# Chunked linear attention and a feed-forward block on one core: block 0's tokens turned from the two rounded parts of y, both halves of W1 centred by mean products, and all pieces in another order

## The chip, the cores and the metric

The kernel runs on 1 core of one Trainium2 chip. The metric is the device time of the program in microseconds (us); lower is better. Before the change the median of three runs is 186.92 us (186.61 to 187.53).

## The reference

```python
# attention: x (4, 8, 768, 32), a (4, 8, 768), B and C (4, 8, 768, 16), chunks of 32 tokens
for c in range(nc):
    la = log_a[:, :, sl]
    cum = np.cumsum(la, axis=-1)
    L = np.exp(cum[:, :, :, None] - cum[:, :, None, :]) * causal
    M = np.einsum('bhin,bhjn->bhij', Cc, Bc) * L
    y_intra = np.einsum('bhij,bhjd->bhid', M, xc)
    y_inter = np.einsum('bhin,bhnd->bhid', Cc, state) * np.exp(cum)[:, :, :, None]
    y[:, :, sl] = y_intra + y_inter
    state = decay_full[:, :, None, None] * state + np.sum(Bx, axis=2)
# feed-forward on the tokens (4, 768, 256): w_ch1 (256, 1024), w_ch2 (1024, 256)
mu, var = np.mean(x, -1, keepdims=True), np.mean((x - mu) ** 2, -1, keepdims=True)
xn = (x - mu) / np.sqrt(var + 1e-06) * g_ln
ch = np.maximum(xn @ w_ch1, 0.0) @ w_ch2
return x + ch
```

Here the x of the second part is the attention's y with the heads side by side. `w_ch1` and `w_ch2` arrive as float64.

## The kernel before

The 768 tokens are cut into six blocks t = 0 to 5 of 128 tokens; a block holds all 4 batches, so its tiles are 128 partitions by 512 columns. Within a block the attention works on two halves of 64 tokens.

**One block of attention.** `scaled_c` and `parted` (pieces C and cm) scale C by a decay and mask it into two tiles; in block 0 `parted_at_once` (cx) does both steps in one instruction. `scaled_b` (B) scales B. `score` (G) multiplies them, `weighted` (R, four instructions) applies the decays held in WW, `entering` and `value` (Vi, V) build y in PSUM from the incoming state and from x, and `carry` (Z), `kept` (K) and `state_of` (S) step the state. The decays of blocks 0 and 1 come from products with a table of sums (e, cum, msps, emps) and exponentials on ScalarE; those of blocks 2 to 5 from a scan whose result goes through HBM (scr) and comes back as the tile ud.

**Feed-forward.** y is held as two float32r parts, yh (rounded) and yl (the rest), and so are both weights. `hidden` (h) forms one 128-row slice of the hidden layer from six products of 512 columns: yh by the upper part of W1, yh by its lower part, yl by its upper part, each over two halves k of the 256 features. `hidden_h` and `hidden_l` (hh, hl) take the relu and split it again; `outputs` (o) and `outputs_of` (oc) multiply by W2; `finished` (oe) scales by the inverse deviation and adds the token. The mean is taken out of W1 instead of out of y: W1 is multiplied by g and by (1 - 1/256), which the text calls centring. W1 has two column halves c = 0 and 1, each in two row halves k. The float64 words are first turned into float32 by pieces k0, k1, k2, k3, kr and f (magnitude, clamped, shifted, signed, rest, whole).

**The centring before.** Half c = 1 is centred by `centred` (wc): for each k two float32 products of 512 columns, one with the tile gd (built by `centring` from the identity, g and -g/256) and one with gneg. Half c = 0 is centred by `mean_of` (wm): two float32 products for both k, and then one VectorE instruction for each k, `less_mean` (wf). `upper` and `lower` (wh, wl) split the result.

**The tokens.** The deviation and the residual need y with tokens on partitions. Blocks 1 to 5 get it by a 32x32 transpose on VectorE and a trip through HBM (tb, bo, bi). Block 0 has `turned` (T): eight TensorE transposes of the float32 copy y32, which four gathers (y) made.

**Order.** A string ISSUE lists every piece in order; each engine runs its instructions in that order, and waits only for data and for buffers. All DMAs are issued by SyncE's queue (SP). The letter after a colon picks the engine. Pieces `fill` are products of zeros that nothing reads; `pc` is a tiny DMA that reads a loaded tile, so that the queue behind it waits for that load. PSUM has eight banks: five for the attention, three (pool ps_ffn) for e, cum, emps, wc, wm, ph and po in turn; a product into a bank waits until its last reader is done.

## Time and profile before

| | before |
|---|---|
| median of three runs | 186.92 us |
| the profiled execution, its own time | 186.59 us |
| its span (first to last instruction) | 184.8 us |
| TensorE matmul busy | 180.0 us, 97% |
| VectorE / ScalarE / GpSimd busy | 141.9 / 63.0 / 44.3 us |
| DMA | 23.66 MB |

Busy time of TensorE counts overlapping matmuls once, so how long one product holds the engine is read from the starts of neighbouring rows, not from its own duration. A float32 product shows as two records (x2), a transpose or a float32r product as one. A name such as ph or yt is the tile that is written, and w, top and yps drop their numbers.

### The profile page before, as it was taken

How to read it: one execution, taken by the hardware profiler on the slowest of the kernel's cores; microseconds unless marked ns; L12 is line 12 of the kernel's file. 1: busy time of each engine (PE TensorE's matmuls, PEld its weight loads, DVE VectorE, ACT ScalarE, POOL GpSimd, SP SyncE). 2: the span in 40 equal slices, each digit the busy share in tenths (PEclk: the TensorE clock that was granted, in tenths of full speed). 3: DMA queues.
4: the chain of work that ended last, by engine and by line, in shares of the span. 5: the costliest groups of instructions: out<-in, count | busy, mean ns of one | idle time of the engine just before them, and what ended most of it. 6: DMA issues, size and time to landing. Idle time of an engine off the chain costs nothing.

```text
span 184.8 us, 6145 instructions
## 1 busy us (share of the span) xinstructions
PE 180.0 (97%) x2674; PEld 150.1 (81%) x2674; DVE 141.9 (77%) x299; ACT 63.0 (34%) x119; POOL 44.3 (24%) x48
## 2 busy tenths in 40 slices
PE   8899999999999999999999999999999999999992
PEld 6666587877899999989779888888888888888892
DVE  0699988999999978897899789684557855587741
ACT  4699587575332382051208110212011310012000
POOL 0004788563232691014830001000020000000000
PEclk9999999999999999999999999999999999999999
DMA  5997235593896867377243280300070005830011
GB/s 147 311 397 298 58 86 178 176 331 130 249 180 151 233 198 199 96 182 186 28 145 61 82 206 4 85 4 4 0 142 0 0 4 172 188 95 0 4 57 57
DMA packets 37745, 23.66 MB, mean 128 GB/s; under 512 B 23350, under 2 KB 31958, under 8 KB 37718
## 3 DMA queue, kind: packets, MB, share of 16 engines
q1 hardware_dynamic: 37718, 23.27, 45.3%
q8 instruction: 21, 0.34, 0.8%
q14 instruction: 6, 0.05, 0.1%
HBM read 17.36 MB, written 5.90 MB: 126 GB/s over the span
## 4 chain that ended last, share of the span: by engine, by line
PE 93%; DMA 2%; SPq 1%; DVE 1%; issue 1%; DVEq 0%
PE ph L542 37%; PE po L562 15%; PE po L563 8%; PE po L568 8%; PE pp L578 6%; PE yps L424 5%; PE G L397 4%; PE yps L416 3%; PE Z L436 3%; DMA b<-in_bn_dram 2%; PE wc L243 2%; PE idle L597 1%; PE wm L248 1%; SPq L167 1%; PE yt L496 0%
## 5 line engine op out<-in xcount | busy, mean ns | idle before, releaser
L542 PE MATMUL ph<-yh,w 128*128 128x512 f32 x192 | 53.0, 398 | 0.0
L547 ACT ACTIVATE hh<-ph 128x512 fp32r<-128x512 f32 x29 | 17.1, 598 | 75.3 <-PE ph L542 69.0
L562 PE MATMUL po<-w,hh 128*128 128x512 f32 x120 | 42.3, 393 | 0.0
L542 PEld LDWEIGHTS ph<-yh,w 128*128 128x128 f32 x192 | 34.4, 188 | 7.8 <-issue 0.7
L553 DVE SCALAR_TENSOR_TENSOR hl<-ph,hh 128x512 fp32r<-128x512 f32 x48 | 32.4, 686 | 8.2 <-ACT hh L547 7.5
L563 PE MATMUL po<-w,hl 128*128 128x256 f32 x120 | 33.8, 282 | 0.0
L542 PE MATMUL ph<-yl,w 128*128 128x512 f32 x96 | 29.7, 391 | 0.0
L562 PEld LDWEIGHTS po<-w,hh 128*128 128x128 f32 x120 | 22.5, 188 | 5.1 <-issue 0.4
L583 DVE SCALAR_TENSOR_TENSOR o<-po,rstd,ytok 128x256 f32<-128x256 f32 x20 | 9.7, 483 | 18.2 <-PE po L563 14.2
L563 PEld LDWEIGHTS po<-w,hl 128*128 128x128 f32 x120 | 22.7, 189 | 0.2
L542 PEld LDWEIGHTS ph<-yl,w 128*128 128x128 f32 x96 | 18.0, 188 | 3.9
L403 DVE TENSOR_TENSOR R<-G,WW 128x512 f32<-128x512 f32 x24 | 15.4, 680 | 2.1 <-PE G L397 1.6
L549 DVE TENSOR_SCALAR hh<-ph 128x512 fp32r<-128x512 f32 x19 | 12.9, 681 | 2.6 <-PE ph L542 2.6
L568 PE MATMUL po<-w,hh 128*128 128x256 f32 x80 | 14.3, 281 | 0.0
L568 PEld LDWEIGHTS po<-w,hh 128*128 128x128 f32 x80 | 12.3, 188 | 0.4 <-issue 0.2
L383 ACT COPY WW<-wt 32x1024 f32<-32x1024 f32 x10 | 10.4, 1040 | 5.0 <-DVE R L403 4.8
L578 PE MATMUL pp<-w,hh 128*128 128x256 f32 x64 | 11.5, 281 | 0.0
L477 POOL TENSOR_TENSOR yl<-y,yh 128x512 fp32r<-128x512 f32 x3 | 3.9, 1294 | 31.5 <-DVE yh L474 31.5
L568 PE MATMUL po<-w,hl 128*128 128x256 f32 x40 | 11.2, 279 | 0.0
L228 POOL TENSOR_TENSOR top<-top,low 128x512 int32<-128x512 int32 x4 | 5.4, 1362 | 22.6 <-DVE top L217 19.4
L462 POOL TENSOR_TENSOR sbd<-S,cst 128x256 f32<-128x256 f32 x6 | 4.1, 689 | 27.0 <-DVE S L452 27.0
L578 PEld LDWEIGHTS pp<-w,hh 128*128 128x128 f32 x64 | 10.0, 188 | 0.4
(105 smaller groups left out, 263.6 us busy)
## 6 DMA issues: line engine op xcount, KB each, us to landing
raw<-in_w_dram SPq DMA_DIRECT2D x8, 512.0 KB, 6.3
xt<-in_x_dram SPq DMA_DIRECT2D x6, 512.0 KB, 7.1
...
```

The costliest lines, as they stand in the source:

```text
L383: e.copy(WW[rows, :, :, 1].rearrange("p b h k -> p (b h) k"), wt[rows, t].unsqueeze(2).to_broadcast([SUB, NR, SUB]))
L403: nc.vector.tensor_tensor(out=R.rearrange("p b i k -> p b (i k)"), in0=tiles.pop(("G", t, q)).rearrange("p b i k -> p b (i k)"), in1=WW.re ...
L424: nc.tensor.matmul(tiles["y", t, g, f][32 * k:32 * k + 32, b], x[r, b * NH + h], tiles["R", t, h // 2][r, b, h % 2], start=(t + f + b == 0 ...
L542: nc.tensor.matmul(ph, W1[m // 4, k][:, s, mc], v[:, k], start=(i == 0), stop=(i == len(cmb) - 1))
L547: e.activation(h, tiles["ph", t, m], AF.Relu)
L549: e.tensor_scalar(out=h, in0=tiles["ph", t, m], scalar1=0.0, scalar2=None, op0=ALU.max)
L553: nc.vector.scalar_tensor_tensor(out=l, in0=tiles.pop(("ph", t, m)), scalar=0.0, in1=tiles["hh", t, m].bitcast(F32), op0=ALU.max, op1=ALU. ...
L562: nc.tensor.matmul(both, tiles["hh", t, m][:, cols], W2[m // 2,][:, :, (m % 2) * DM:(m % 2 + 1) * DM], start=(m == 0), stop=False)
L563: nc.tensor.matmul(both[:, 0], tiles["hl", t, m][:, cols], W2[m // 2,][:, 0, (m % 2) * DM:(m % 2 + 1) * DM], start=False, stop=(m == MC - 1))
L568: nc.tensor.matmul(po, tiles[v, t, m][:, cols], W2[m // 2,][:, s, (m % 2) * DM:(m % 2 + 1) * DM], start=(n == 0), stop=(n == len(cmb) - 1))
L578: nc.tensor.matmul(tiles["po", t, b], tiles[v, t, m][:, cols], W2[m // 2,][:, s, (m % 2) * DM:(m % 2 + 1) * DM], start=(c + n + b % 2 == 0 ...
L583: nc.vector.scalar_tensor_tensor(out=o, in0=tiles.pop(("po", t, b)), scalar=tiles["rstd", t][:, b], in1=tiles["ytok", t][:, b], op0=ALU.mu ...
```

## The change

Four things change in the code. `centred` and the tile gd go, and half c = 1 of W1 is centred by `mean_of` and `less_mean` like half c = 0. `turned` forms block 0's tokens as ordinary products of yh and of yl with a float32r identity (identr, made by the new piece `ir`), summed in PSUM: sixteen float32r products of 128 columns in place of eight transposes; the four gathers into y32 for block 0 go with it. `hidden` can be issued in two parts: the two products of yh with the upper W1 first, the other four later. And the tile cs gets two buffers. ISSUE lists the pieces in a new order with new engines for some.

```diff
-    gd = hp.tile([P, KC, P], F32, tag="hh", name="gd")
+    identr = cp.tile([P, P], F32R, name="identr")
...
+    def rounded_ones(e=nc.gpsimd):
+        e.tensor_copy(identr, ident) if e is not nc.scalar else e.copy(identr, ident)
...
-            for k in range(KC):
-                e.activation(gd[:, k], ident, AF.Identity, bias=gneg[:, k:k + 1], scale=gt[:, k:k + 1])
...
-    def centred(c, k):
-        w = centre[c, k] = ps_ffn.tile([P, 512], F32, tag="ffn", name=f"wc{c}{k}")
-        for n, j in enumerate((k, 1 - k)):
-            nc.tensor.matmul(w, gd[:, k] if j == k else gneg[:, j:j + 1].to_broadcast([P, P]), f32[1, c, j], start=(n == 0), stop=(n == 1))
...
-        cs = tiles["cs", t] = p1.tile([P, TB], F32, tag="cs", name=f"cs{t}")
+        cs = tiles["cs", t] = p2.tile([P, TB], F32, tag="cs", name=f"cs{t}")
...
-                nc.tensor.transpose(ps[:, v, g * P:(g + 1) * P], tiles["y32", t][:, g, tok], ident)
+                for n, part in enumerate(("yh", "yl")):
+                    nc.tensor.matmul(ps[:, v, g * P:(g + 1) * P], tiles[part, t][:, g, tok], identr, start=(v + g + n == 0), stop=(v + g + n == 3))
...
-    def hidden(t, m):
+    def hidden(t, m, *part):
...
         for i, (s, v, k) in enumerate(cmb):
-            nc.tensor.matmul(ph, W1[m // 4, k][:, s, mc], v[:, k], start=(i == 0), stop=(i == len(cmb) - 1))
+            if not part or (i < KC) == (part[0] == 0):
+                nc.tensor.matmul(ph, W1[m // 4, k][:, s, mc], v[:, k], start=(i == 0), stop=(i == len(cmb) - 1))
...
-ld la, l1, fill 8 256, fill 4 256, fill 2 256, ini, ld sums, ld mask, ld w1 1 0, l2, lr 0, fill 6 256, e 1, x 1, dc 0, fill 5 256, fill 3 64, so,
+ld la, l1, l2, inv, ld sums, fill 2 256, fill 1 512, fill 8 256, ld mask, lr 0, ini, ld w1 1 0, ones, e 1, x 1, W:v 0, ld g, dc 0, lr 1, k0 1 1 0,
```

The first place is VectorE at the start, from the tile of decayed B (bs) to the weighted scores R of block 0. Before:

```order
L363 SCALAR_TENSOR_TENSOR cm_163<-c_158,cst,ud_149 128x512 x2
L367 TENSOR_TENSOR bs_168<-b_166,ud_149 128x512
L217 SCALAR_TENSOR_TENSOR top_147<-raw_123,top_147 128x512
L348 TENSOR_TENSOR cs_223<-c_158,ud_149 128x512
L228 ISA top_147<-top_147,low_211 128x1024
L203 TENSOR_SCALAR top_219<-top_219 128x512
L313 TENSOR_TENSOR mblk<-msum,selt 32x144
L212 TENSOR_SCALAR top_219<-top_219 128x512
L376 TENSOR_TENSOR be_236<-bt_226,pend 128x512
L217 SCALAR_TENSOR_TENSOR top_219<-raw_216,top_219 128x512
L403 TENSOR_TENSOR R_265<-G_175,WW 128x512
```

And now:

```order
L342 TENSOR_TENSOR cs_154<-c_146,ud_148 128x512
L361 TENSOR_TENSOR bs_166<-b_151,ud_148 128x512
L212 TENSOR_SCALAR top_143<-top_143 128x512
L307 TENSOR_TENSOR mblk<-msum,selt 32x144
L217 SCALAR_TENSOR_TENSOR top_143<-raw_127,top_143 128x512
L228 ISA top_143<-top_143,low_170 128x1024
L203 TENSOR_SCALAR top_178<-top_178 128x512
L397 TENSOR_TENSOR R_230<-G_197,WW 128x512
L397 TENSOR_TENSOR R_242<-G_194,WW 128x512
L212 TENSOR_SCALAR top_178<-top_178 128x512
L397 TENSOR_TENSOR R_255<-G_196,WW 128x512
```

The two cm have gone to ScalarE, be to GpSimd, and the R stand earlier: between them and behind them lie the steps of the second W1 tile (top_219 before, top_178 now).

The second place is TensorE at the start, between the sums of decays (e, cum, msps) and the scores G. Before:

```order
L293 MATMUL cum_133<-cf,lr_126 128x128 x4
L597 MATMUL idle<-const-float32-0.0 128x256
L597 MATMUL idle<-const-float32-0.0 128x64
L306 MATMUL msps<-cst,la 32x8 x6
L597 MATMUL idle<-const-float32-0.0 128x512
L293 MATMUL cum_170<-cf,lr_156 128x128 x4
L397 MATMUL G_175<-cm_163,bs_168 64x128
```

And now:

```order
L287 MATMUL cum_136<-cf,lr_123 128x128 x4
L300 MATMUL msps<-cst,la 32x8 x6
L595 MATMUL idle<-const-float32-0.0 128x256
L275 MATMUL e_181<-la,cf 128x192
L287 MATMUL cum_183<-cf,lr_141 128x128 x4
L391 MATMUL G_194<-cm_164,bs_166 64x128
```

The product e_181 (e 0) stood behind G before and stands ahead of it now, in the bank of cum_136, so it waits until ScalarE has read that tile twice; two fills have moved behind G.

The third place is TensorE where block 0's feed-forward begins. Before:

```order
L243 MATMUL wc_409<-top_219,gd 128x512
L243 MATMUL wc_409<-top_147,gneg 128x512
L248 MATMUL wm_422<-top_287,gneg 128x512
L248 MATMUL wm_422<-top_298,gneg 128x512
L496 MATMUL yt_425<-cst,y_373 128x128 x4
L496 MATMUL yt_434<-cst,y_373 128x128 x4
L436 MATMUL Z_450<-xt_234,be_236 32x64 x16
```

And now:

```order
L242 MATMUL wm_423<-top_279,gneg 128x512
L242 MATMUL wm_423<-top_288,gneg 128x512
L540 MATMUL ph_426<-yh_361,w_364 128x512
L540 MATMUL ph_426<-yh_361,w_416 128x512
L540 MATMUL ph_429<-yh_361,w_364 128x512
L540 MATMUL ph_429<-yh_361,w_416 128x512
L491 MATMUL yt_432<-identr,yh_361 128x128
L491 MATMUL yt_432<-identr,yl_362 128x128
```

The first four products of ph stand ahead of the turned tokens yt, which are now float32r products of the two parts; the pair yh, yl comes eight times.

## Rows read from the trace of the kernel before

**Rows 1.** All waits of TensorE: total us, times, longest

```profile
PE idle L597 <- PEq L688: 0.8, 1, 0.8
PE cum L293 <- ACT msum L309: 0.6, 1, 0.6
PE G L397 <- DVE bs L367: 0.2, 1, 0.2
```

**Rows 2.** Busy time by stretch: length, busy us (count) per engine, clock, DMA

```profile
10.09:24.40 14.31, 14.31 (x381) 8.85 (x381) 14.12 (x31) 11.28 (x30) 6.76 (x8) 1.00 0.59 222
24.40:181.60 157.20, 157.16 (x2253) 134.72 (x2248) 122.76 (x260) 45.56 (x80) 37.33 (x36) 1.00 0.44 114
```

**Rows 3.** Timeline of TensorE at the start: start us, length us, instruction, count [idle before]

```profile
0.78 3.75 PE L597 MATMUL idle<-const-float32-0.0 128*128 128x256 f32 x8 [0.78 <-PEq L688]
...
4.93 1.06 PE L293 MATMUL cum<-cf,lr 128*128 128x128 f32 x8
5.82 0.77 PE L597 MATMUL idle<-const-float32-0.0 128*128 128x256 f32 x4
...
10.09 1.21 PE L397 MATMUL G<-cm,bs 32*64 32x128 f32 x64 [0.20 <-DVE bs L367]
...
13.47 0.65 PE L436 MATMUL Z<-xt,be 64*32 64x64 f32 x32
...
14.48 1.13 PE L243 MATMUL wc<-top,gd 128*128 128x512 f32 x2
...
16.45 0.69 PE L416 MATMUL yps<-c,sbd 32*64 32x64 f32 x32
...
18.66 1.13 PE L243 MATMUL wc<-top,gd 128*128 128x512 f32 x2
...
20.48 1.88 PE L248 MATMUL wm<-top,gneg 128*128 128x512 f32 x4
22.20 1.04 PE L496 MATMUL yt<-cst,y 128*128 128x128 f32 x8
23.16 1.30 PE L436 MATMUL Z<-xt,be 64*32 64x64 f32 x96
24.40 1.19 PE L542 MATMUL ph<-yh,w 128*128 128x512 f32 x4
...
27.34 1.21 PE L397 MATMUL G<-cm,bs 32*64 32x128 f32 x64
```

**Rows 4.** The chain that ended last: start us, us, what

```profile
67.23 2.80 PE po L568 x24
...
159.54 10.89 PE ph L542 x48
```

**Rows 5.** Timeline of ScalarE

```profile
6.52 0.67 ACT L198 ACTIVATE top<-raw 128x512 f32<-128x512 f32 x1 [1.06 <-DMA raw<-in_w_dram]
7.09 0.59 ACT L299 ACTIVATE ud<-cum 128x512 f32<-128x512 f32 x1
...
23.37 1.34 ACT L356 ACTIVATE cm<-cs,cst 128x512 f32<-128x512 f32 x2 [2.10 <-POOL cs L348]
```

**Rows 6.** Timeline of VectorE

```profile
13.85 2.46 DVE L403 TENSOR_TENSOR R<-G,WW 128x512 f32<-128x512 f32 x4
16.24 0.40 DVE L203 TENSOR_SCALAR top<-top 128x512 f32<-128x512 f32 x1
...
22.40 0.75 DVE L252 SCALAR_TENSOR_TENSOR top<-top,gt,wm 128x512 f32<-128x512 f32 x1
```

**Rows 7.** DMA issues of the page: count, size, median us to landing

```profile
raw<-in_w_dram SPq DMA_DIRECT2D x8, 512.0 KB, 6.3
```

**Rows 8.** Timeline of SyncE's queue: start us, time to issue, DMA

```profile
4.00 0.43 SPq L157 DMA_DIRECT2D raw<-in_w_dram  x1
...
28.73 3.05 SPq L144 DMA_DIRECT2D ud<-scr  x2
```

**Rows 9.** Timeline of GpSimd: the wait for block 2's decays

```profile
32.75 1.28 POOL L348 TENSOR_TENSOR cs<-c,ud 128x512 f32<-128x512 f32 x1 [0.42 <-DMA ud<-scr]
```

More of the change, by code (lines that the diff above doesn't have):

```diff
@@ L232, in centring @@
             e.activation(gneg, gt, AF.Copy, scale=-1.0 / DM)
-            for k in range(KC):
-                e.activation(gd[:, k], ident, AF.Identity, bias=gneg[:, k:k + 1], scale=gt[:, k:k + 1])
         else:
             e.tensor_scalar(out=gneg, in0=gt, scalar1=-1.0 / DM, scalar2=None, op0=ALU.mult)
-            for k in range(KC):
-                e.tensor_scalar(out=gd[:, k], in0=ident, scalar1=gt[:, k:k + 1], scalar2=gneg[:, k:k + 1], op0=ALU.mult, op1=ALU.add)
-    def centred(c, k):
-        w = centre[c, k] = ps_ffn.tile([P, 512], F32, tag="ffn", name=f"wc{c}{k}")
-        for n, j in enumerate((k, 1 - k)):
-            nc.tensor.matmul(w, gd[:, k] if j == k else gneg[:, j:j + 1].to_broadcast([P, P]), f32[1, c, j], start=(n == 0), stop=(n == 1))
     def mean_of(c):
@@ L534, in inverse @@
         nc.vector.reciprocal(rstd, rstd)
-    def hidden(t, m):
+    def hidden(t, m, *part):
         yh, yl = tiles["yh", t], tiles["yl", t]
-        ph = tiles["ph", t, m] = ps_ffn.tile([P, TB], F32, tag="ffn", name=f"ph{t}{m}")
+        if ("ph", t, m) not in tiles:
+            tiles["ph", t, m] = ps_ffn.tile([P, TB], F32, tag="ffn", name=f"ph{t}{m}")
+        ph = tiles["ph", t, m]
         cmb = [(s, v, k) for s, v in ((0, yh), (1, yh), (0, yl)) for k in range(KC)]
@@ L606, in linear_attention_ffn @@
     do = dict(
-        ld=load, pc=after, fill=fill, fillb=fill_small, az=restart, ini=initial, inv=cleared, ones=masks, gm=centring,
+        ld=load, pc=after, fill=fill, fillb=fill_small, az=restart, ini=initial, inv=cleared, ones=masks, gm=centring, ir=rounded_ones,
         lr=logs_repeated, dc=since_middle, du=decay_from_middle, rcl=rest_clipped, ru=rest_since, riv=rest_last, rd=rest_till, ro=rest_out, C=scaled_c, cm=parted, cx=parted_at_once, B=scaled_b, c2=inter, be=ended,
@@ L610, in linear_attention_ffn @@
         W=decays, G=score, R=weighted, Vi=entering, V=value, Z=carry, K=kept, S=state_of, sb=diagonal,
-        k0=magnitude, k1=clamped, km=bounded, k2=shifted, k3=signed, kr=rest, f=whole, wc=centred, wm=mean_of, wf=less_mean, wh=upper, wl=lower,
+        k0=magnitude, k1=clamped, km=bounded, k2=shifted, k3=signed, kr=rest, f=whole, wm=mean_of, wf=less_mean, wh=upper, wl=lower,
         y=gathered, yh=upper_y, yl=lower_y, uy=upper_of, ly=lower_of, T=turned, tc=tokens, tb=blocks_turned, bo=blocks_out, bi=blocks_in, st=stats, ag=aggregate, rs=root, rc=inverse,
```

72 lines of the change are left out of this document (36 added, 36 removed).

## Prediction

> **What bounds the kernel.** I read TensorE's waits first: there are three, 1.6 us together, and none behind the first G [rows 1]. The table by stretch says the same: from the first G to the first ph TensorE is busy for 14.31 of 14.31 us, and from there to its last product for 157.16 of 157.20 us [rows 2]. So from 10.1 us on nothing ends later than TensorE's own queue. A faster VectorE or ScalarE buys nothing; the change can gain only by products that are gone, or by an earlier start of the dense part, and every new wait of TensorE costs its full length. The second stretch holds the products for all six blocks, and these stay the same in number and size. What has to be priced is the road to them. VectorE, too, is busy for 14.12 of the first stretch's 14.31 us [rows 2], so there the two engines run side by side, and I follow both.
>
> **Prices.** From start to start a float32 product of 512 columns takes 0.86 us (wm: 20.48 to 22.20 for two). The four of wc took 14.48 to 16.45 and 18.66 to 20.48, 3.79 us [rows 3]. Float32r products take 0.227 us at 512 columns (10.89 / 48) and 0.117 at 256 (2.80 / 24) [rows 4]; the straight line through both gives 0.062 at 128, where the trace has none. Vi and V together take 2.21 us, G by its own length 1.2, Z and emps 1.01, the two Z behind the turned tokens 1.24 [rows 3]. The first h behind such small products costs 0.1 more, and the six products of one h 1.4 to 1.5: twelve products fill 24.40 to 27.34 [rows 3].
>
> **What goes from TensorE.** Two wc pairs, 3.79 us, are replaced by one wm pair, 1.72: 2.07 saved. The turned tokens are eight transposes now, 0.96 us (22.20 to 23.16), and become sixteen products, 16 x 0.062 = 0.99 by the line: nothing gained or lost. The bound from above is the price of a plain float32 product of 128 columns, (5.82 - 4.93) / 4 = 0.22 us [rows 3], 3.5 us in all; from below sixteen products cannot cost under nothing, which would gain 0.96. I take the line, since both its points are float32r. The Trainium skill (TensorE: Matmul & The Clock Gate, section "Back-to-back issue gap") gives about 81 ns per product for a stream of weight load and product at 128 columns; by it the sixteen would take 1.3 us and the sum would be 0.3 us worse. The same page (section "Terms") calls transpose mode four times faster for FP32, which speaks against giving it up; here the transposes' 0.12 us stand against 0.22 for plain float32, under a factor of two, and float32r needs no such help.
>
> **The first step, to G.** In the old order G waits for bs on VectorE, behind two cm there, and starts at 10.09 [rows 1, 3]. In the new one the decay tile ud is ready at 7.68 as before (7.09 + 0.59), cs takes some 0.7 on VectorE, like the R or wf [rows 6], until 8.4, and the two cm 1.34 on ScalarE [rows 5], until 9.8; bs is done by 9.1 beside them. G starts at about 9.85, 0.25 earlier. TensorE gets nothing done meanwhile: e 0 waits for both readings of cum (the second ends near 8.2), and fills of 512 and 64 columns have gone behind G, so it idles some 1.8 us ahead of G against 0.8 before [rows 1].
>
> **The second step, to the last float32 product.** Behind G come fills of 512, 64 and 256 columns, emps, Z, and fills of 512 and 256: with half a float32 product's 0.86 for each 256 columns, and 0.1 at two changes of shape, that is 1.2 + 1.5 + 1.0 + 1.3 = 5.0, so TensorE is at the first product of wm 1 at 14.9 and through it at 15.75. The second needs the tile top of W1's lower row half. Its load is now one place later in SP's queue: landing was 4.0 + 6.3 = 10.3 by the median [rows 7, 8], and I take 10.5 (between 10.3, if only the full queue counts, and 10.8, if the delay is passed on whole). On ScalarE it is then k0 to 11.2; on VectorE k1 (0.4), four R at 0.6 with a k2 between, k3 0.6, another k1, and f 0.7 [rows 6]: 11.2 + 0.4 + 2.8 + 0.6 + 0.4 + 0.7 = 16.1. So wm 1 waits 0.3 us and ends at 17.0; Vi and V end at 19.2, against 18.66 before. VectorE goes on from 16.0 with k2, k1, k2, two k3, two wf (0.7 each) and f: 0.4 x 3 + 1.2 + 1.4 + 0.7 = 4.5, so the second product of wm 0 starts at 20.45 instead of 20.1, and wm 0 ends at 21.3, against 22.20 before.
>
> **The third step, to block 1's G.** Then come four h products (1.0), the turned tokens with a change of shape (1.1), Z (1.24) and ten h products (2.4 with the extra change): 21.3 + 5.8 = 27.1. By then fourteen h products are done. The old order is at the same G at 27.34 with twelve; the two are worth 0.46. **Gain: 0.24 + 0.46 = 0.7 us.** The four inputs of this stretch, the rest yl, the lower part of W1, the second wf of c = 0 and the next block's cm, come from VectorE and ScalarE 0.1 to 0.5 us ahead of TensorE by the same adding. The gathers for block 0, four on ScalarE, and the two gd were covered by TensorE's queue already, so their going is worth nothing by itself. The wf pair that VectorE gains (2 x 0.7) is already in the 4.5 us.
>
> **The rest.** Behind 27 us I take the old rate, since the products are the same and the old stretch has no waits. A bank of ps_ffn is free again after its hl, which by my adding comes 0.5 to 3 us ahead of need up to Z of block 2. I cannot read from any row that the order of blocks 2 to 5 is as free of waits; each that appears is a loss.
>
> **Sum.** 186.59 (the profiled execution) - 0.7 = 185.9. The median of the runs stands 0.33 above that execution, so I forecast 186.2 for the median, 0.4% under 186.92. About 0.5%, 0.93 us, is what a measurement of this kernel can tell from no change.
>
> **Rivals.**
> *More of the saving arrives.* If VectorE and the load are each some 0.3 us earlier than I added them, both wm waits go (0.3 + 0.35), and the gain is 1.3 us: 185.6. If even the idle time ahead of G were no longer than before, it would be 2.1: 184.8. For it: VectorE's slots scatter by 0.1 us, and I add some twenty. Against it: VectorE is full in that stretch. Chance 0.36 for a gain over 0.93.
> *The turned tokens run at the float32 price.* Sixteen at 0.22 make 3.5 us, 2.5 more, with all of h behind them: 188.7. For it: no row has float32r at 128 columns. Against it: the two sizes that are there lie on one line. It decides from 0.10 us a product on, where the gain is gone. Chance 0.10.
> *A wait that the old order had on GpSimd holds VectorE.* Block 2's cs needs ud, which goes through HBM; GpSimd waited for it, 0.42 us, until 32.75, and ud was issued at 28.73 [rows 8, 9]. It is VectorE's now, ahead of yh of block 1 and of the hl that frees a bank. By my adding VectorE comes to it at 31.8 and the bank is needed 1.5 us after its hl would end, so a landing at 32.75 still costs TensorE nothing; beyond 33.3 each us costs one. If ud takes the 6.3 us of a weight load [rows 7] instead of the 4 it took, TensorE loses 1 to 2: 187.2 to 188.2, slower. For it: larger loads stand close behind it in SP's queue. Against it: they are issued later. Chance 0.08.
> *The clock falls.* The granted clock is 1.00, 2.4 GHz, in both stretches [rows 2]; but the first four fills of 256 columns took 3.75 us, over 0.9 each, where half of a 512 takes 0.43 [rows 3], so the start is at the lower level, 1.2 GHz. If the 1.8 us of idling ahead of G bring that level back, G and what follows take double for as long as those fills did, 3.75 us, of which half is lost: 188.1. Against it: 0.8 us of idling there did nothing before. Chance 0.06.
>
> **Numbers.** My forecast, a gain of 0 to 0.93 us, has 0.40; its own range is 185.9 to 186.9. Faster by over 0.5% has 0.36, slower by over 0.5% 0.10 + 0.08 + 0.06 = 0.24. Under 185.1 lies only the full saving, some 0.05; above 188.0 the float32 price and the far end of the others, some 0.14. So the range is 185.1 to 188.0.
>
> **What would show it.** G at 9.8 to 9.9 with TensorE idle by 1.8 us ahead of it; a TensorE wait of some 0.3 us in wm 1 for top and one in wm 0; wc gone; yt sixteen records in about 1.0 us; block 1's G at 27.1; no waits behind. I am wrong if yt takes over 1.6 us, if ph or po wait for VectorE's yh or hl, or if any stretch behind G is below clock 1.00.

## The result and the profile after

The changed kernel takes 188.61 us (median of nine runs, 187.41 to 189.33); beside it the kernel before took 186.66. The ratio is 1.009, with an interval of 1.0071 to 1.0108: slower by 0.9%, where I had forecast 186.2 us, in a range of 185.1 to 188.0. The profiled execution took 188.66 us, its span is 186.9 us against 184.8. TensorE is busy for 180.6 us of it, VectorE for 140.1, ScalarE for 70.0, GpSimd for 40.2.

All waits of TensorE in the changed kernel (total us, times, longest); [rows 1] answers to it:

```profile
PE e L275 <- ACT msum L303: 0.8, 1, 0.8
PE Z L430 <- DMA xt<-in_x_dram: 0.8, 1, 0.8
PE idle L595 <- PEq L686: 0.8, 1, 0.8
PE wm L242 <- POOL top L228: 0.4, 1, 0.4
PE G L391 <- ACT cm L350: 0.2, 1, 0.2
```

Two waits are new behind G: Z waits for xt's load, and wm for a tile that GpSimd writes. The first is not in the prediction. The second is there in part: the prediction had a wait in wm 0, but at its second product and for VectorE (and one in wm 1, which did not come). The timeline of TensorE at the start, to be laid beside [rows 3]:

```profile
9.97 1.21 PE L391 MATMUL G<-cm,bs 32*64 32x128 f32 x64 [0.20 <-ACT cm L350]
...
14.32 0.65 PE L430 MATMUL Z<-xt,be 64*32 64x64 f32 x32 [0.79 <-DMA xt<-in_x_dram]
...
16.30 2.04 PE L242 MATMUL wm<-top,gneg 128*128 128x512 f32 x4
18.27 0.69 PE L410 MATMUL yps<-c,sbd 32*64 32x64 f32 x32
18.90 1.48 PE L418 MATMUL yps<-R,xt 64*32 64x64 f32 x128
20.78 2.32 PE L242 MATMUL wm<-top,gneg 128*128 128x512 f32 x4 [0.40 <-POOL top L228]
22.54 1.49 PE L540 MATMUL ph<-yh,w 128*128 128x512 f32 x4
23.87 0.22 PE L491 MATMUL yt<-identr,yh 128*128 128x128 f32 x1
23.92 0.27 PE L491 MATMUL yt<-identr,yl 128*128 128x128 f32 x1
...
25.69 1.31 PE L430 MATMUL Z<-xt,be 64*32 64x64 f32 x96
...
29.46 0.85 PE L391 MATMUL G<-cm,bs 32*64 32x128 f32 x38
```

The reader is to see three things. wm 0 starts at 20.78, no earlier than the old 20.48, although TensorE has a float32 pair less ahead of it; its second product, the last two of the four records, starts 1.20 us later still, where 0.96 would do (what the first product behind V takes in the kernel before, from 18.66 to 19.62). The same view from 21.95 us on:

```profile
21.98 1.12 PE L242 MATMUL wm<-top,gneg 128*128 128x512 f32 x2
```

The sixteen turned products take 1.82 us (23.87 to 25.69), 0.113 each. And block 1's G comes at 29.46 with fourteen h products done; the old order was there at 27.34 with twelve, which with two more (0.46) is 27.8. So 1.7 us of the 2.1 by which the span is longer are there before G.

The timeline of VectorE in the changed kernel, ahead of wm 0's inputs:

```profile
14.21 1.35 DVE L217 SCALAR_TENSOR_TENSOR top<-raw,top 128x512 int32<-128x512 int32 x1
...
18.30 1.29 DVE L217 SCALAR_TENSOR_TENSOR top<-raw,top 128x512 int32<-128x512 int32 x2
19.51 1.40 DVE L246 SCALAR_TENSOR_TENSOR top<-top,gt,wm 128x512 f32<-128x512 f32 x2
20.82 1.10 DVE L228 CUSTOM_DVE_ANT_0 top<-top,low 128x1024 uint16<-128x1024 uint16 x1
```

And that of GpSimd:

```profile
13.97 1.04 POOL L365 TENSOR_TENSOR c<-cs,em 128x512 f32<-128x512 f32 x1
19.13 1.59 POOL L228 TENSOR_TENSOR top<-top,low 128x512 int32<-128x512 int32 x1 [4.12 <-DVE top L217]
...
20.76 0.61 POOL L438 TENSOR_TENSOR K<-S,emt 128x256 f32<-128x256 f32 x1
```

wm 0's first product needs the sum f of W1[0,0] (L228 on GpSimd, until 20.72), its second the f of W1[0,1] (L228 on VectorE, until 21.92). One k3 (L217) takes 1.35 us where two others take 1.29 together, and that f takes 1.10 where such a one takes 0.69 elsewhere; in both cases GpSimd is in an operation of its own (c at 13.97, K at 20.76). The experiments turn on that.

A second profile of the same kernel, taken later, shows how much of this is one execution's.

> The changed kernel unaltered, profiled a second time. If Z's 0.8 us wait for xt was one execution's (the other kernels with the same start and the same order of loads had none), Z starts at 13.3 to 13.6 without it, wm 0 still starts at 20.3 to 20.8 behind GpSimd's f, its second product at 21.5 to 22.0 behind VectorE's, and block 1's G at 29.0 to 29.5. If the wait belongs to the order of loads, it is there again with 0.5 us or more.

It took 187.29 us (span 185.5; the kernel before 186.47 beside it). Its waits of TensorE behind the first product:

```profile
PE wm L242 <- POOL top L228: 0.5, 1, 0.5
PE G L391 <- ACT cm L350: 0.2, 1, 0.2
```

And wm 1 and wm 0 in its timeline, the second product of wm 0 in a view that starts behind the first:

```profile
15.52 1.91 PE L242 MATMUL wm<-top,gneg 128*128 128x512 f32 x4
...
19.96 2.32 PE L242 MATMUL wm<-top,gneg 128*128 128x512 f32 x4 [0.49 <-POOL top L228]
...
21.15 1.12 PE L242 MATMUL wm<-top,gneg 128*128 128x512 f32 x2
```

Z's wait is gone, the wait of wm for GpSimd is there again; the second product starts 1.19 us behind the first. The first G stands at 10.05, that of block 1 at 28.64.

The second profile lets the 2.07 us be followed that TensorE is spared. From G to wm 1 the way is 5.47 us (10.05 to 15.52), where the old order took 4.39 to its first wc (10.09 to 14.48): 1.1 us more, since more fills stand there. At wm 0, 0.49 and 0.23 us are waits. So wm 0 ends only some 0.2 us earlier than the old one. Then the turned tokens take 0.85 us more than the old transposes, and G of block 1 is 0.8 us behind the old order's 27.8.

Both profiles show that loss of 0.8 us. What comes on top differs: the runs of the changed kernel span 185.5 to 187.6 us, those of the old one mostly 184.6 to 185.6. In the first profile it is Z's wait of 0.8 ahead of G and 0.4 behind it; the median run is as long as that one, but whether it loses its time in the same places isn't shown.

### The profile page after: what moved, and what is told of

Same layout as the page of the kernel before. It is cut to its first block, busy times and chain, and to the rows that moved or that the text cites. A ratio compares the mean times of both kernels' runs of the same rounds, so it can differ in the third digit from the quotient of the medians.

```text
span 186.9 us, 6145 instructions
## 1 busy us (share of the span) xinstructions
PE 180.6 (97%) x2678; PEld 149.7 (80%) x2678; DVE 140.1 (75%) x292; ACT 70.0 (37%) x133; POOL 40.2 (22%) x42
## 4 chain that ended last, share of the span: by engine, by line
PE 87%; DMA 6%; DVE 3%; SPq 1%; issue 1%; ACT 0%
PE ph L540 37%; PE po L560 15%; PE po L566 8%; PE po L561 8%; DMA raw<-in_w_dram 6%; PE pp L576 6%; PE yps L418 4%; PE G L391 3%; PE yps L410 3%; PE Z L430 2%; PE yt L491 1%; DVE top L228 1%; DVE top L217 1%; SPq L167 1%; PE wm L242 1%
## 5 line engine op out<-in xcount | busy, mean ns | idle before, releaser
L540 PE MATMUL ph<-yh,w 128*128 128x512 f32 x192 | 53.9, 400 | 0.0
L545 ACT ACTIVATE hh<-ph 128x512 fp32r<-128x512 f32 x35 | 20.9, 597 | 61.5 <-PE ph L540 59.1
L547 DVE TENSOR_SCALAR hh<-ph 128x512 fp32r<-128x512 f32 x13 | 8.9, 683 | 2.2 <-PE ph L540 1.6
L438 POOL TENSOR_TENSOR K<-S,emt 128x256 f32<-128x256 f32 x8 | 5.5, 687 | 21.4 <-DVE S L446 21.4
L518 DVE BATCH_NORM_STATS2 st<-ytok 128x6 f32<-128x256 f32 x24 | 9.5, 411 | 0.0
L576 PE MATMUL pp<-w,hl 128*128 128x256 f32 x32 | 8.9, 279 | 0.0
```

What stands on the lines that cost most here:

```text
L518: nc.vector.bn_stats(out=st, in_=tiles["ytok", t][:, b])
L540: nc.tensor.matmul(ph, W1[m // 4, k][:, s, mc], v[:, k], start=(i == 0), stop=(i == len(cmb) - 1))
L545: e.activation(h, tiles["ph", t, m], AF.Relu)
L547: e.tensor_scalar(out=h, in0=tiles["ph", t, m], scalar1=0.0, scalar2=None, op0=ALU.max)
L576: nc.tensor.matmul(tiles["po", t, b], tiles[v, t, m][:, cols], W2[m // 2,][:, s, (m % 2) * DM:(m % 2 + 1) * DM], start=(c + n + b % 2 == 0 ...
```

## Experiments

Each ratio is to the kernel before, with its interval; the changed kernel has 1.009. A diff of the string ISSUE shows only the pieces around those that move. The expectations speak of four theories. **A:** the read on SP's queue, moved ahead of the loads, makes them late, and that sets the time. **B:** a turned product costs 0.113 us, its weight load, and the sixteen are paid in full. **C:** the chain of VectorE and GpSimd to wm 0's inputs, not TensorE's queue, sets wm 0, so that what TensorE is spared ahead of it becomes waiting. **D:** a VectorE operation with its operands in SBUF is held while GpSimd works, and that lengthens the chain of C.

**The loads.** The read that holds SP's queue goes back behind the loads (in the changed kernel), or ahead of them (in the old one).

```diff
-sp, pc 4 w1 1 0, ld bt 0, be 0,
+sp, ld bt 0, be 0,
...
-ld x 0, ld w1 0 0, k2 1 1 1, ld w1 0 1,
+ld x 0, ld w1 0 0, k2 1 1 1, ld w1 0 1, pc 4 w1 1 0,
```

> The changed kernel with one thing undone: the small read of W1[1,0] that holds SP's queue stands behind the loads of xt and of the upper half of W1 again. Theory A (the held queue made xt, and the loads behind it, late): xt lands at 12.6 instead of 14.2, Z of block 0 starts at about 13.1 without the 0.8 us wait, W1's c = 0 tiles come 1.2 us earlier too, wm 0 ends at 21.4 instead of 22.5, block 1's G starts at about 28.2 instead of 29.5, and the time is 1.2 us less than the changed kernel's: 0.2 to 0.7 us above before, a ratio of 1.001 to 1.004. Rival (the transfers share one bandwidth, so that starting one earlier makes another late): block 1's G stays at 29.3 to 29.5 and the ratio at 1.009.

Measured: 1.0109 (1.0085 to 1.0132). xt's load is issued at 5.44 instead of 7.83, Z no longer waits for it, and nothing is won. The earlier loads seem not to be free: W1's first tile reaches ScalarE at 7.05 instead of 6.59, and G starts at 10.35 instead of 9.97. Two later kernels with the early load of xt have 10.12 and 10.40, the kernels with the held queue 9.82 to 10.10, one execution each. And wm 0 waits for GpSimd as before. The clock fell in this profile (last section), but was at 0.997 or above in the other five runs, which took 188.5 to 189.1 us. Theory A falls as the cause of the time; Z's wait is real but not what sets wm 0.

```diff
-C:v 0, f:v 1 1 0, ld bt 0, k1 1 1 1,
+C:v 0, f:v 1 1 0, pc 4 w1 1 0, ld bt 0, k1 1 1 1,
...
-R 0 2, pc 4 w1 1 0, S 0 0,
+R 0 2, S 0 0,
```

> The kernel before with the small read of W1[1,0] on SP's queue moved ahead of bt's load, where the changed kernel has it, and nothing else. Theory A: bt and xt land 1.5 us later (12.8 and 14.2 instead of 11.2 and 12.6), be on VectorE and Z on TensorE wait for them, Z of block 0 starts at 14.3 or later instead of 13.47, VectorE's work for W1 is pushed back by as much, and the time is 1 to 2 us above before, a ratio of 1.005 to 1.011. Rival (the loads have slack in the old order): within 0.3 us, 1.000 to 1.002.

Measured: 1.0034 (1.0020 to 1.0047), between the two. Z starts at 13.57, 0.1 later than before, and G of block 1 at 27.50; the profiled run loses its 0.9 us at 55 us, in pp, where the profile names no releaser. That doesn't bear out theory A either; the 0.3% that the interval leaves has no cause shown.

**The price of the turned tokens.** In the changed kernel yl's eight products are left out; in the old one the turned tokens alone are changed, and stand behind the last yl, which they now read.

```diff
-                for n, part in enumerate(("yh", "yl")):
+                for n, part in enumerate(("yh",)):
```

> The changed kernel with block 0's tokens turned from yh alone, eight float32r products instead of sixteen (the yl part is left out of them). Theory B (each costs 0.113 us, what loading its 128 weight columns takes, not the 0.062 of the line): the eight take 0.9 us instead of 1.8, block 1's G starts 0.9 us earlier, and as TensorE is full behind it the time is 0.9 us less than the changed kernel's, a ratio of 1.004. Rival one, the price of the prediction (0.062, the rest of the 1.8 us being change of shape): 0.5 us less, 1.0065. Rival two (the wait for W1's parts behind them takes it back): G of block 1 unmoved, 1.009.

Measured: 1.0051 (1.0027 to 1.0076). The row of the eight in that kernel, and the next:

```profile
23.50 1.00 PE L491 MATMUL yt<-identr,yh 128*128 128x128 f32 x8
24.43 1.30 PE L430 MATMUL Z<-xt,be 64*32 64x64 f32 x96
```

0.93 us for eight, 0.116 each with the change of shape, and the time falls by 0.0039 x 186.7 = 0.7 us: what theory B expects, though the intervals of the two kernels overlap.

```diff
-                nc.tensor.transpose(ps[:, v, g * P:(g + 1) * P], tiles["y32", t][:, g, tok], ident)
+                for n, part in enumerate(("yh", "yl")):
+                    nc.tensor.matmul(ps[:, v, g * P:(g + 1) * P], tiles[part, t][:, g, tok], identr, start=(v + g + n == 0), stop=(v + g + n == 3))
...
-uy:v 0 0 0, wl:v 1 1 0, ly 0 0 0, ly 0 1 0, wf 0 0,
+uy:v 0 0 0, ly 0 0 0, ly 0 1 0, T 0 0, T 0 1, wl:v 1 1 0, wf 0 0,
```

> The kernel before with the turned tokens alone changed: sixteen float32r products from yh and yl behind the last yl, no gathers of block 0's y on ScalarE. Theory B: yt takes 1.82 us instead of 0.97, with a wait of at most 0.3 us ahead for yl; TensorE is full from there on, so the time is 0.85 to 1.1 us above before, a ratio of 1.0045 to 1.006. Rival, the price of the prediction (sixteen in 1.0 us): 1.000 to 1.002.

Measured: 1.0078 (1.0044 to 1.0113). yt takes 2.22 us (22.18 to 24.40), 0.35 of it a wait, and from G to G the order is 0.83 us longer (28.62 - 10.54 against 27.34 - 10.09). That is theory B's size, and the interval shuts out the 1.000 to 1.002 of the prediction's price. The profiled run is longer than its kernel's median: of the 2.9 us by which its span exceeds the old one's, 0.83 are these, 0.45 lie ahead of G, and 1.4 are two waits without a releaser, in ph (0.4) and pp (1.0).

**The mean products alone.** The kernel before with only the centring changed.

```diff
-k0 1 0 1, wc 1 0, kr 1 0 0,
+k0 1 0 1, wm 1, wf 1 0, kr 1 0 0,
...
-f:v 1 0 0, wc 1 1, y 0 0 0,
+f:v 1 0 0, wf 1 1, y 0 0 0,
```

> The kernel before with the centring alone changed: wm 1 in place of the first wc pair, no second wc pair, and the two wf of c = 1 on VectorE, one right behind wm 1, one where the second pair stood. Theory C (VectorE, full in that stretch, takes the place of TensorE as the bound): VectorE has 1.3 us more to do, f of W1[0,0] is done at 20.6 as TensorE has been idle from 18.6 on, wm 0 starts at 20.6 with a wait of some 2 us ahead of it, block 1's G is 0 to 1.0 us later than the old 27.34, and the ratio is 1.000 to 1.006. Rival (the 2.07 us of TensorE's work come out at the end): wm 0 at 18.7, G at 25.3, ratio 0.989.

Measured: 1.0109 (1.0082 to 1.0136), worse than either theory. The timeline of TensorE at wm 0:

```profile
21.17 3.10 PE L246 MATMUL wm<-top,gneg 128*128 128x512 f32 x4 [2.36 <-DVE top L228]
```

And of VectorE, the f that it waits for:

```profile
20.34 0.69 DVE L228 CUSTOM_DVE_ANT_0 top<-top,low 128x1024 uint16<-128x1024 uint16 x1
```

The 2.07 us that TensorE no longer works it waits, and 0.3 more, for VectorE's f; the wf pair comes on top for all that follows, and G of block 1 is at 30.00. In the old order those inputs come hardly sooner than they are needed: the f of GpSimd, for the second product (about 21.3 there), ends at 21.09.

```profile
19.50 1.59 POOL L228 TENSOR_TENSOR top<-top,low 128x512 int32<-128x512 int32 x1 [3.15 <-ACT em L324]
```

Part of the time of the mean products alone is the clock's, though: the page's PEclk falls to 0.7 to 0.8 in two slices after the wait, and of the six runs the four with a mean clock of 0.989 to 0.991 take 188.87 to 189.74 us, the two at 1.000 187.90 and 188.55.

Does VectorE alone keep the saving in? Here four of its operations ahead of wm 0 are left out.

```diff
-k1 1 0 0, k2 1 0 0, k3 1 0 0, k1 1 0 1, k2 1 0 1, k3 1 0 1, kr 1 0 1,
+k1 1 0 0, k1 1 0 1, kr 1 0 1,
```

> The kernel before with the mean products alone (b2), and four operations of VectorE left out ahead of wm 0: k2 and k3 of W1[0,0] and of W1[0,1] (their weights keep their clamped top words instead of the value, so the output is off). Theory C (VectorE's chain alone keeps the 2.07 us of TensorE from coming out): 2.0 us less on VectorE, so f of W1[0,0] ends at 18.8 to 19.2 instead of 21.0, wm 0 starts at 18.8 to 19.3 with a wait under 0.5 us instead of 2.4, its second product at 19.9 to 20.3, block 1's G at 26.0 to 26.6, and the ratio falls from b2's 1.011 to 0.992 to 0.997, under before. Rival (the loads, ScalarE or the gathers hold the stretch as well): ratio 1.000 or above.

Measured: 1.0017 (0.9994 to 1.0040), 1.7 us under the kernel it is derived from (part of which is that kernel's clock), though not under before, where 0.992 to 0.997 was expected. The timeline of TensorE in this kernel:

```profile
18.57 2.17 PE L246 MATMUL wm<-top,gneg 128*128 128x512 f32 x4
...
21.55 0.65 PE L434 MATMUL Z<-xt,be 64*32 64x64 f32 x32
22.80 1.12 PE L434 MATMUL Z<-xt,be 64*32 64x64 f32 x64 [0.60 <-issue]
```

Of VectorE:

```profile
20.85 1.51 DVE L259 TENSOR_TENSOR w<-top,w 128x512 fp32r<-128x512 f32 x1
22.29 0.74 DVE L486 TENSOR_TENSOR yl<-yps,yh 128x256 fp32r<-128x256 f32 x2
```

And of GpSimd:

```profile
20.54 1.28 POOL L346 TENSOR_TENSOR cs<-c,ud 128x512 f32<-128x512 f32 x1
```

wm 0 starts 2.6 us earlier and without a wait, 1.9 us ahead of the old order's, as theory C has it. Then Z stops, and takes 2.30 us instead of 1.24: by the code it needs banks that the yl free, and the yl stand behind a wl that takes 1.51 us while GpSimd makes cs. G of block 1 comes at 26.80, 0.5 ahead of the old one, and the span is the old 184.8: the rest of the lead goes behind G, with no wait that the profile shows. So VectorE's chain is what wm 0 waits for; that the 2.07 us would come out at the end without it is not shown.

**VectorE held by GpSimd.** The same pattern, made on purpose: two additions on GpSimd that nothing needs, in the old order where it idles.

```diff
+        e.tensor_tensor(out=idler, in0=src[:, :512], in1=src[:, 512:1024], op=ALU.add)
...
-c2:p 0,
+c2:p 0, xx, xx,
```

> The kernel before with two additions on GpSimd, behind its c2 of block 0, where it idles from 16.35 to 19.5 us: each adds two stretches of WW (128x512, 1.3 us alone) into a tile that nothing reads. Theory D (an operation of VectorE whose operands lie in SBUF alone doesn't proceed while GpSimd's runs, it ends about its own length after it; one that reads PSUM isn't held): k2 and one or two of the k behind it take 1.0 to 1.5 us instead of 0.4 to 0.7, f of W1[0,0] ends 1.5 to 2.2 us later than 19.95, wm 0 and all behind it come 1.0 to 2 us later, and the ratio is 1.005 to 1.011. Rival (the two engines run side by side, and what was read as holding was something else): no operation of VectorE is longer, ratio 1.000.

Measured: 1.0100 (1.0068 to 1.0131). VectorE in this kernel:

```profile
16.70 1.40 DVE L212 TENSOR_SCALAR top<-top 128x512 int32<-128x512 int32 x1
18.14 1.65 DVE L217 SCALAR_TENSOR_TENSOR top<-raw,top 128x512 int32<-128x512 int32 x1
```

GpSimd in it, the two additions:

```profile
16.32 2.91 POOL L378 TENSOR_TENSOR idler<-WW 128x512 f32<-128x512 f32 x2
```

The same two in the kernel before, with GpSimd idle:

```profile
16.68 0.43 DVE L212 TENSOR_SCALAR top<-top 128x512 int32<-128x512 int32 x1
17.14 0.69 DVE L217 SCALAR_TENSOR_TENSOR top<-raw,top 128x512 int32<-128x512 int32 x1
```

k2 and k3 are 0.97 and 0.96 us longer, wm 0 starts at 22.06 instead of 20.48, G of block 1 at 29.20. Theory D holds. The Trainium skill (SBUF — State Buffer, section "Who interferes with whom") states the rule: a VectorE instruction with two SBUF inputs, or in a two-port mode, and a GpSimd instruction that reads SBUF exclude each other, and the later "fully blocks". The trace agrees (1.40 and 1.65 us beside GpSimd, 0.43 and 0.69 without), and also where an operand is in PSUM: the R of [rows 6] take 0.6 each, though GpSimd's f runs from 14.07 to 15.34. It speaks against this change, and the prediction overlooked it.

**Trying to bring wm 0's inputs forward.** In the changed kernel the two f go ahead of what stands in front of them; then both to VectorE.

```diff
-k0 1 0 1, k2 1 0 0, kr 1 0 1, kr 1 0 0, k1 1 0 1, k2 1 0 1, fill 6 256, k3 1 0 0, f 1 0 0, k3 1 0 1,
+kr 1 0 0, k0 1 0 1, k2 1 0 0, k3 1 0 0, f 1 0 0, kr 1 0 1, k1 1 0 1, k2 1 0 1, fill 6 256, k3 1 0 1,
...
-wf 1 0, Vi 0, V 0 0,
+f:v 1 0 1, wf 1 0, Vi 0, V 0 0,
...
-wf 1 1, az, f:v 1 0 1, pc 2 w1 0 0,
+wf 1 1, az, pc 2 w1 0 0,
```

> The changed kernel with the sixteen products kept and the two sums f of W1's upper half put ahead of what stood in front of them: GpSimd's f of W1[0,0] (1.6 us) starts behind a k3 that VectorE does 1.3 us earlier, and VectorE's f of W1[0,1] goes ahead of the two wf. Theory C (wm 0 is set by these two sums, not by TensorE's queue or by the loads): wm 0's first product starts at 19.5 to 19.9 instead of 20.4 to 20.8 with no wait, the second follows without the 0.2 us gap, wm 0 ends at 21.3, block 1's G comes about 1.0 us earlier, and the ratio to before is 1.0025 to 1.005. Rival (the loads of W1's upper half, late behind the held queue, set it): k1 of W1[0,0] starts at 15.3 to 16.1 as before and nothing in front of it is won, wm 0 stays at 20.4, and the ratio at 1.007 to 1.009.

Measured: 1.0175 (1.0141 to 1.0209). VectorE in this kernel:

```profile
17.71 1.46 DVE L212 TENSOR_SCALAR top<-top 128x512 int32<-128x512 int32 x1
19.20 0.98 DVE L217 SCALAR_TENSOR_TENSOR top<-raw,top 128x512 int32<-128x512 int32 x1
20.32 1.33 DVE L228 CUSTOM_DVE_ANT_0 top<-top,low 128x1024 uint16<-128x1024 uint16 x1
```

And GpSimd:

```profile
17.49 1.32 POOL L228 TENSOR_TENSOR top<-top,low 128x512 int32<-128x512 int32 x1 [3.57 <-DVE top L217]
...
18.86 0.78 POOL L438 TENSOR_TENSOR K<-S,emt 128x256 f32<-128x256 f32 x1
19.60 1.50 POOL L370 TENSOR_TENSOR be<-bt,pend 128x512 f32<-128x512 f32 x1
```

The clock fell in this execution (0.55 from 23.50 to 28.00 us), behind the rows shown here. Moved forward, GpSimd's f, K and be meet k2, k3 and f on VectorE instead of the two wf, which read PSUM: each is held, 2.0 us together. wm 0's first product came at 19.43 as expected, the second only behind VectorE's f.

```diff
-k3 1 0 0, f 1 0 0, k3 1 0 1, ld bt 1,
+k3 1 0 0, f:v 1 0 0, k3 1 0 1, f:v 1 0 1, ld bt 1,
...
-wf 1 1, az, f:v 1 0 1, pc 2 w1 0 0,
+wf 1 1, az, pc 2 w1 0 0,
```

> The changed kernel with both sums f of W1's upper half on VectorE, each right behind its k3, so that GpSimd has no long operation there. Theory C and D together (wm 0 is set by GpSimd's 1.6 us for the one f and by the other, held behind GpSimd's K): f of W1[0,0] ends at 19.5 and that of W1[0,1] at 20.7 instead of 20.4 to 20.7 and 21.6 to 21.9, wm 0 has no wait for GpSimd, its second product starts at 20.7 to 21.0 instead of 21.6 to 22.0, and block 1's G comes 0.5 to 0.8 us earlier: ratio 1.005 to 1.0065 against the changed kernel's 1.009. Rival (the two wf that come 0.6 us later hold wh and the first h): G unmoved, 1.009.

Measured: 1.0171 (1.0129 to 1.0213). GpSimd, free of f, took K and be earlier, and be (17.26, 1.32 us) held a k2 for 0.75.

With that, the read of SP's queue behind x's load, the k0 of W1[0,0] ahead of Z, and VectorE's f of W1[1,1] ahead of the next k1:

```diff
-k3 1 0 0, f 1 0 0, k3 1 0 1,
+k3 1 0 0, k3 1 0 1, f:v 1 0 0, f:v 1 0 1,
...
-sp, pc 4 w1 1 0, ld bt 0, be 0,
+sp, ld bt 0, be 0,
...
-ld x 0, ld w1 0 0, k2 1 1 1,
+ld x 0, pc 4 w1 1 0, ld w1 0 0, k2 1 1 1,
...
-du 1 1, Z 0 0, R 0 1, S 0 0, k0 1 0 0,
+du 1 1, k0 1 0 0, Z 0 0, R 0 1, S 0 0,
```

> The changed kernel, sixteen products kept, with all that wm 0 waits for made early: the read that holds SP's queue behind xt's load, ScalarE's k0 of W1[0,0] ahead of S, VectorE's k3 and f of W1[1,1] ahead of k1 of W1[0,0], both f of the upper half on VectorE and ahead of the two wf. If the loads, VectorE's order and GpSimd together are the whole of what held wm 0, its first product starts when V ends, at 19.4 to 19.9, without a wait, wm 0 ends at 21.2 to 21.6 instead of 22.2 to 22.5, the first four h have no wait, block 1's G starts at 27.8 to 28.3, and the ratio is 1.000 to 1.003, the rest being the turned tokens. Rival (something else, such as h's own inputs, takes the wait over): wm 0 early, but G at 29 or later and the ratio at 1.007 or above.

Measured: 1.0176 (1.0138 to 1.0214). The k0 and the loads were early, wm 0 started at 20.75 all the same: be again held a k2 (1.30 us instead of 0.42), and TensorE waited 1.0 us for VectorE's f.

With transposes instead of the sixteen products, and gathers on ScalarE, in the changed order and then in that of the run above:

```diff
+                nc.tensor.transpose(ps[:, v, g * P:(g + 1) * P], tiles["y32", t][:, g, tok], ident)
...
-wh 1 1 1, ld c 1, ir:a, W 1, wm 0,
+wh 1 1 1, ld c 1, y 0 0 1, y 0 1 1, y 0 0 0, y 0 1 0, W 1, wm 0,
```

> The changed kernel with block 0's tokens turned as before: y gathered by four copies on ScalarE (in the place of the rounded identity, ahead of the copies of WW) and eight transposes. Theory B (a turned product costs 0.113 us as a transpose does, and there were sixteen of them): yt takes 0.97 us instead of 1.82, block 1's G comes 0.85 us earlier, the time is 0.8 us under the changed kernel's, a ratio of 1.0045 to before. Rival (ScalarE's 1.0 us of copies delays WW and the tokens, and with them the statistics or block 1's R): the ratio stays at 1.009.

Measured: 1.0125 (1.0096 to 1.0155). The four copies start only at 23.26: ScalarE is done with wh at 21.6 and waits 1.66 us, by the profile for VectorE's yl. So yt waited 0.7 us for y. The rival came true.

```diff
-uy 0 0 1, wh 1 1 0, ld as,
+uy 0 0 1, y 0 0 1, y 0 0 0, uy 0 0 0, wh 1 1 0, ld as,
...
-wh 1 1 1, ld c 1, ir:a, W 1, wm 0,
+wh 1 1 1, y 0 1 1, y 0 1 0, em 1, ld c 1, W 1, wm 0,
```

> The kernel of e5 with the tokens turned by eight transposes again, the four copies of y on ScalarE between its copies of yh. Theory B: 0.85 us less of TensorE's time than in e5, all of it in front of a full queue, so 0.85 us less in all: block 1's G at 27.0 to 27.4 with fourteen h done, and a ratio of 0.996 to 0.999, faster than both kernels. Rival (ScalarE's copies come late, as where they stood behind wh): yt waits for y, and the ratio is that of e5 or above.

Measured: 1.0148 (1.0105 to 1.0192), a median of 189.52 us against the 190.14 of the kernel that it is derived from, which the intervals don't tell apart; the second h waited 1.0 us for ScalarE's em, which had moved behind the copies of y. And the old order with VectorE relieved by GpSimd (and wh of the first half later):

```diff
-C:v 0, f:v 1 1 0, ld bt 0,
+C 0, f 1 1 0, ld bt 0,
...
-k0 1 0 1, wc 1 0, kr 1 0 0,
+k0 1 0 1, wm 1, kr 1 0 0,
...
-f:v 1 0 0, wc 1 1, y 0 0 0,
+f:v 1 0 0, wf 1 0, wf 1 1, y 0 0 0,
```

> The kernel before with the mean products alone, and VectorE relieved where it is full: cs of block 0 and f of W1[1,0] on GpSimd, which idles till 14 us there, and both wf of c = 1 behind f of W1[0,0]. Theory C: with 1.2 us taken off VectorE and the two wf out of the way, f of W1[0,0] is done at about 19.5, wm 0 starts at 19.5 to 19.7 instead of 20.48, with a wait of some 1 us left ahead of it, and what was won (0.7 to 0.9 us) stays to the end: a ratio of 0.995 to 0.996. Rival (the saving of the centring never comes out, since the loads and ScalarE are at the limit too): 0.999 to 1.003.

Measured: 1.0124 (1.0102 to 1.0146). cs and f on GpSimd held VectorE's k3 (9.71, 1.75 us) and mblk (11.84, 1.37 us; 0.29 in the kernel before): what was taken off VectorE came back as holds. None of these six beats either kernel.

**Slack or a full queue ahead of wm 0?** The changed kernel with both wc pairs back and no wf of c = 1.

```diff
-ld x 1, wm 1, wf 1 0, Vi 0,
+ld x 1, wc 1 0, Vi 0,
...
-wf 1 1, az, f:v 1 0 1, pc 2 w1 0 0, V 0 1,
+az, f:v 1 0 1, pc 2 w1 0 0, V 0 1, wc 1 1,
```

> The changed kernel with the two wc pairs back for c = 1 and no wf of it on VectorE, all else as in the changed kernel (the identity's load and gd a little earlier): TensorE has 2.07 us more to do, VectorE 1.33 us less. Theory C (TensorE has that much slack ahead of wm 0, since it waits there for VectorE and GpSimd): wm 0 starts at 21.2 to 21.5 without a wait instead of 20.4 to 20.8 with one, the first four h have no wait, block 1's G comes at 29.4 to 29.9, and the ratio is 1.009 to 1.012. Rival (TensorE's queue is the bound, as the prediction had it for V and what follows): 1.7 to 2.1 us more, 1.018 to 1.020.

Measured: 1.0220 (1.0197 to 1.0242). The run tells nothing apart: gd on ScalarE put k0 of W1[0,0] off until 15.88, and VectorE's chain with it. So it was repeated with gd out of the way, k0 at 14.46.

```diff
-sp, pc 4 w1 1 0, ld bt 0,
+sp, ld id, pc 4 w1 1 0, ld bt 0,
...
-du 1 1, Z 0 0, R 0 1, S 0 0, k0 1 0 0, k3 1 1 1,
+gm:a, Z 0 0, R 0 1, S 0 0, k0 1 0 0, du 1 1, k3 1 1 1,
```

> As the run with the two wc pairs back in the changed kernel, but with the identity loaded ahead of bt and gd made on ScalarE where it idles, so that ScalarE's S and k0 of W1[0,0] are not pushed back by gd as they were there (1.0 us). Theory C (TensorE has slack ahead of wm 0 in the changed kernel, since it waits there for VectorE and GpSimd): k1 of W1[0,0] at 15.3 as in the changed kernel, V ends at 19.4 to 19.8, wm 0 starts at 21.2 to 21.6, 0.6 to 1.0 us later than in the changed kernel although TensorE has 2.07 us more to do, and the ratio is 1.010 to 1.014. Rival (TensorE's queue is the bound): wm 0 at 22.4 or later with every start of VectorE as in the changed kernel, ratio 1.018 or above.

Measured: 1.0230 (1.0186 to 1.0274), the rival's ratio and 2.6 us over the changed kernel. The timeline of TensorE at wm 0:

```profile
21.47 1.88 PE L250 MATMUL wm<-top,gneg 128*128 128x512 f32 x4
```

There is no wait. That is 0.7 us later than in the first profile of the changed kernel, but 1.5 later than in the second, with 2.07 more on TensorE ahead of it: the slack is 0.6 us there, about the wait of 0.49, and 1.4 at most. So theory C holds for a part only. In the new order most of what the mean products save does reach wm 0, and with the pairs back it is lost again. Behind wm 0 the second h waits 0.5 us for a wl, the last reader of a wc bank, and there are waits behind G in Z and po without a releaser.

Last, less work for VectorE in the new order:

```diff
-k0 1 0 1, k2 1 0 0, kr 1 0 1, kr 1 0 0, k1 1 0 1, k2 1 0 1, fill 6 256, k3 1 0 0, f 1 0 0, k3 1 0 1, ld bt 1,
+k0 1 0 1, kr 1 0 1, kr 1 0 0, k1 1 0 1, fill 6 256, f 1 0 0, ld bt 1,
```

> The changed kernel with k2 and k3 of W1[0,0] and W1[0,1] left out (their weights keep their clamped top words instead of the value, so the output is off): 2.0 us less on VectorE ahead of wm 0, GpSimd's f of W1[0,0] bound by ScalarE's rest (18.3) instead of by VectorE. Theory C and D: that f ends at 19.9, VectorE's f of W1[0,1] is held by it and ends at 20.5 instead of 21.6 to 21.9, wm 0 starts at 19.9 and its second product at 20.8, the first four h have no wait, block 1's G comes at 28.2 to 28.7 with the sixteen turned products, and the ratio is 1.003 to 1.006 against 1.009. Rival (TensorE's queue, the loads or ScalarE set it): G at 29.1 or later, ratio 1.008 or above.

Measured: 1.0082 (1.0052 to 1.0113). The timeline of TensorE at wm 0:

```profile
19.76 1.98 PE L242 MATMUL wm<-top,gneg 128*128 128x512 f32 x4
```

The waits at wm 0 are gone, as theory C has it, and G of block 1 comes at 28.11. That is 1.35 us earlier than in the changed kernel's first profile, but only 0.53 earlier than in the second, and the time can't be told from the changed kernel's. In this execution the lead is lost behind G:

```profile
PE po L566 <- issue: 0.5, 1, 0.5
PE ph L540 <- POOL yl L471: 0.4, 1, 0.4
PE Z L430 <- issue: 0.2, 1, 0.2
```

> The changed kernel with k2 and k3 of the upper half left out, profiled a second time. If the waits behind block 1's G that gave back its lead (ph for GpSimd's yl, po and Z with no releaser shown) belong to the order, they are there again at the same products and the span is 1.3 us or more over what G's start would give with the changed kernel's 157.4 us behind it; if they were one execution's, G is again at 28.0 to 28.4 and the span 185.4 to 186.0.

It took 187.81 us (span 186.0). The three waits are gone, so they are not the order's; instead be held VectorE's k1 at 11.59 (1.28 us instead of 0.42), wm 1 waited 0.9 us, and G came at 28.62, where the changed kernel's second profile has 28.64. wm 0 had no wait in either execution, so its waits come from that chain; but what they are worth at G, 0.0 to 1.35 us, lies within what one kernel's executions differ by.

## Why the prediction was wrong

**To G.** Forecast 9.85, measured 9.97, and 9.82 to 10.10 in the other kernels with this order. Right, though TensorE idled 1.0 us ahead of it in the first profile and 0.2 in the second, not 1.8. From G to 181 us the granted clock is 1.00 in both profiles of the changed kernel.

**To the end of wm 0: the step that failed first.** I had wm 0's second product at 20.45 and the four h behind it done by 22.3. The product came at 21.98 in the first profile and at 21.15 in the second, the h were done by 23.87 and 23.04. Three things in the sum were missing. The first product's input was followed on VectorE alone, though the new order gives f of W1[0,0] to GpSimd, where it takes 1.59 us. The holds were priced at nothing: 0.4 us on f of W1[0,1] in both profiles of the changed kernel, 0.67 on a k3 in the first. (In the second profile that f ends at 21.09 and the product that reads it starts at 21.15; without the hold it could start at 20.92, 0.96 behind the first, and then GpSimd's f is the bound.) And the loads of bt, xt and the upper half of W1, which stand behind the moved read, were not priced, only that of W1's lower row half: Z waited 0.8 us for xt in one profile of two. Undoing that alone gained nothing. In the old order the 2.07 us that TensorE is spared turn into waiting whole, 2.36 us with the mean products alone, and there it is VectorE's chain: with four of its operations left out wm 0 comes 2.6 us earlier and without a wait. In the new order only 0.7 of them became waits at wm 0 (second profile); another 1.1 went into the longer way to wm 1, of which the prediction had counted 0.6: wm 1, forecast at 14.9 with a wait of 0.3, came without one at 15.52, as G, Z, emps and the fills take 5.5 us, not 5.0.

**The turned tokens: a mis-sized term.** Sixteen at 0.062 made 0.99, 1.1 with a change of shape; they took 1.82, over the 1.6 that I had named as a sign of being wrong. At 128 columns a float32r product costs 0.113, about as much as one of the old transposes (0.96 / 8 = 0.12) and as a float32r product of 256 columns (0.117). So the straight line through 512 and 256 does not hold at 128. The Trainium skill (TensorE: Matmul & The Clock Gate, section "LDWEIGHTS (loading the stationary operand)") puts a weight load at its columns over 1.2 in ns, by which I estimate 107 for 128. The trace's 0.113 is close to that, and here each product loads 128 new columns; that the weight load is the reason fits the rows, but no run varies it alone. I had looked only at the same page's figure for a stream (section "Back-to-back issue gap"), 81 ns, which these float32r products don't reach. The upper bound, 0.22, was held.

**Behind G.** G of block 1 was forecast at 27.1: 1.57 of the 2.36 us it is late are wm 0's, 0.72 the turned tokens', the rest small; in the second profile 0.74 and 0.73 of 1.54. From there the first profile takes 157.4 us to the end of its span and the second 156.9; the old order took 157.5 with two h products more to do, 0.46. So the old rate held in the second, and the first lost 0.4 there.

**The rivals.** The rival on the turned tokens pointed at the right term: its turning point, 0.10 us a product, was passed. But the price is not float32's, 0.113 instead of 0.22, and it makes 0.7 us over my sum instead of 2.5. The measured median, 188.61, lies close to that rival's 188.7 by chance: most of what it is over my forecast comes from elsewhere. The wait for ud cost TensorE nothing (VectorE waited for it 0.18 us in the second profile). The clock did not fall here, though TensorE's idling brought it down in other kernels (below). That the new order's time scatters by 1.9 us where the old one's scatters by 1.3 (nine runs each) was in no rival.

What stays open: of the 1.95 us between the medians the two profiles share 0.8; where the median run loses the rest is known for the first profile only. And the waits behind G that show no releaser (pp, po, ph, Z) come and go between executions of one kernel; I have no run that tells their cause.
